# A second block's D stage ahead of the MLP, weights in ten steps, and copies moved between ScalarE and VectorE

## The chip, the cores and the metric

The kernel runs on one core of a Trainium2 chip. A core has five engines that matter here, each with its own in-order queue: TensorE (PE in the profile, its weight loads PEld), VectorE (DVE), ScalarE (ACT), GpSimd (POOL) and SyncE (SP), which only issues DMAs. The metric is the device time of one execution in microseconds; smaller is better. A time is the median of several executions.

## The reference

The input x is (8, 3072, 256) in float32. Along the sequence each of the 8 batches is filtered in the frequency domain, and the result goes through a two-layer MLP with a softplus between the layers, token by token:

```python
X = np.fft.rfft(x, axis=1)
y = np.fft.irfft(X * (filt_r + 1j * filt_i)[None], n=3072, axis=1)
h = y.reshape(8 * 3072, 256) @ w_in                      # (.., 2048)
g = np.maximum(h, 0.0) + np.log1p(np.exp(-np.abs(h)))
out = g @ w_out                                          # (.., 256)
```

The weights w_in (256 x 2048) and w_out (2048 x 256) are float64 in memory.

## The kernel before

**Arithmetic.** Every float32 operand of a matmul is split into two parts in a format that TensorE takes, a rounded high part "hi" and a rest "lo" (names ending in h and l in the profile: inh and inl, dih and dil, zh and zl, gh and gl). A product is three matmuls, hi x hi, lo x hi and hi x lo (`split_mm`, line 73). Making the parts is a copy (hi) and a subtraction (lo) on one of the elementwise engines; `hi_lo` (lines 81 to 86) is given the engine of each. The float64 weights are loaded raw and taken apart with integer and float instructions on VectorE (`weight`, lines 344 to 371: a magnitude copy on ScalarE, then five VectorE instructions, lines 356 to 368), and finished in `weight_ends` (a copy on ScalarE, line 382, and two GpSimd instructions, lines 383 and 384). There are 16 blocks of weights: 0 to 7 of w_in, 8 to 15 of w_out. `together` converts blocks in pairs, with their instructions taking turns.

**The filter** of a batch has four stages. A (12 visits): sums and differences of two halves of x, split, matmuls with the constants ca, evacuated by ScalarE into the DRAM tensor s1. B (13 visits): rows of s1 are loaded (tile bi), split, multiplied by small constants (psb in PSUM), and then by the filter on VectorE (lines 183 to 187) with a GpSimd addition (line 188). C (13 visits): split again (zh, zl), matmuls back (psc), evacuated by ScalarE (co) and written to the DRAM tensor s2. D (four visits and two y visits for each block of 512 tokens; a batch has 6 blocks): a block of s2 is loaded (tile di), split, and multiplied by constants cd with the data as the stationary operand (psd); sums and differences give y, whose parts are the tiles yT, the input of the MLP. `engines(blk)` names the engines of the splits in D: ScalarE with VectorE for batch 0's block 0, ScalarE with GpSimd for block 1, VectorE with GpSimd elsewhere.

**The MLP** works in steps: a step is one block of 512 tokens and 256 of the 2048 hidden columns; there are 8 steps to a block, 48 to a batch, 384 in all (`STEPS`). The first 16 steps take blocks 0 and 1 of batch 0 in turn, four steps each, so that the second half of the weights is needed later. `mm1` computes h (12 matmuls) into one of two PSUM buffers, and ScalarE takes it through three activations in place in the tile s (Abs, line 287; Exp, 288; Ln, 289). `soft` adds max(h, 0) on VectorE (line 296), copies to gh (line 298: on ScalarE for the 48 steps of batch 0, on VectorE later) and subtracts to gl (line 300); the five VectorE instructions of a weight conversion are laid between these three. `mm2` adds the products with w_out into the PSUM tile o, of which there is one buffer, two steps behind; after the last step of a block (and after half a block for the first two) o is evacuated into ob: one half by VectorE (line 324), the other by ScalarE (line 325), or, at the end of the first two blocks, by two VectorE additions.

**Order.** The order of every engine's instructions is written out by hand (a manual schedule). Batch 0 begins with its own A, B and C ahead of the MLP (`first_a`, `first_bc`) and D of block 0 (`first_d`). Then each step has two slots, q = 2s and 2s + 1: mm1 and the ends of a weight in the first, mm2 of step s - 2 and soft in the second; each slot then does the visits listed for it in `slots`. The D visits of a block lie in slots of the block before it; A, B and C of batch b + 1 in the steps of batch b (for batch 1 B and C come one to each free slot, later about two to three). `Run.ahead` issues loads up to 8 slots and splits up to 4 slots ahead of a visit, as far as buffers allow. `WEIGHTS` lists the weight blocks that are converted in each of the first steps; a block is loaded two steps earlier into a buffer that `TAGS` takes from the ring of another tile ("ob" by default; each has 2 buffers, "in" 3), on SP's queue, which waits where the buffer is still in use.

Of the kernel before, what the change touches and what calls it, by code (L numbers as in the profile page):

```python
# [38 lines left out]
STEPS = [(g, 4 * half + i) for half in range(2) for g in range(2) for i in range(4)]  # L39
STEPS += [(g, i) for g in range(2, NB * NBLK) for i in range(NSTEP)]  # L40

WEIGHTS = (9,), (10,), (11,), (4,), (5,), (6,), (7,), (12,), (13,), (14,), (), (15,)

TAGS = {3: "ca", 8: "ca", 5: "ca", 6: "ca", 12: "cd", 7: "in", 13: "in", 14: "in", 15: "in"}

START, END = 480, 504

# [4 lines left out]
def fft_mlp(ctx: ExitStack, tc: tile.TileContext, x, fr, fi, ca, ca0, cb, cc, cd, w_in, w_out, out):  # L52
    nc = tc.nc
# [41 lines left out]
    class Batch:  # L95
# [31 lines left out]
        def a_prep(self, i):  # L127
            self.a_sum(i)
            st = self.t.pop(("as", i))
            self.t["ap", i] = hi_lo(st, P, "in", nc.scalar if self.b == 1 else nc.vector, nc.gpsimd)  # L130

        def a_mm(self, i):
            _, cat = self.t.pop(("a", i))
# [29 lines left out]

        def b_prep(self, u):
            p = self.filled(u)
            hi_eng, lo_eng = self.engines(0)
            src = self.t["b", u][0]
            self.t["bp", u] = hi_lo(src[:p], p, "in", hi_eng, lo_eng if u < 3 or u % 2 else nc.gpsimd)

# [23 lines left out]

        def c_mm(self, u):
            if u == 0:
                self.s2 = dram.tile([2, P, N2, D], F32, tag="s2", name="s2")
            p = self.rows(u)
            zs = self.t.pop(("z", u))
            ps = ps_f.tile([P, 512], F32, tag="f", name="psc")
            if u:  # L200
                split_mm(ps, [cc_sb[:, 0, k] for k in range(2)], zs)
            else:
                for j in range(2):
                    s = slice(256 * j, 256 * j + 256)
                    split_mm(ps[:, s], [cc_sb[:, 1 - j, k] for k in range(2)], [zs[k][:, s] for k in range(2)])
            co = work.tile([P, 512], F32, tag="ao", name="co")
            nc.scalar.activation(out=co[:p], in_=ps[:p], func=AF.Copy)
            nc.scalar.dma_start(
                out=self.s2.rearrange("h m n d -> (m n) h d")[120 * u:120 * u + p],
                in_=co[:p].rearrange("p (h d) -> p h d", h=2),  # L210
            )

        def e_load(self, blk):
            cdt = work.tile([P, 2, 2, 2, P], F32R, tag="cd", name="cd")
# [3 lines left out]
        def d_load(self, i):  # L218
            blk = i // 4
            if ("e", blk) not in self.t:  # L220
                self.e_load(blk)
            dt = work.tile([P, 2, 2, D], F32, tag="di", name="di")
            for h in range(2):
                nc.sync.dma_start(out=dt[:, h], in_=self.s2[h, :, 2 * blk:2 * blk + 2, :])
            self.t["d", blk] = dt, self.t.pop(("e", blk))

        def d_prep(self, i):
            blk, j, c = i // 4, i % 2, i // 2 % 2
            if c == 0:
                dt = self.t["d", blk][0]  # L230
                self.t["dp", blk, j] = hi_lo(dt[:, :, j], P, "di", *self.engines(blk), (2, D))

        def d_mm(self, i):

# [57 lines left out]
    def soft(s, between):  # L292
        h, a = g_of.pop(s)
        hi = mlp.tile([P, 2, 512], F32R, tag="gh", name="gh")
        lo = mlp.tile([P, 2, 512], F32R, tag="gl", name="gl")
        nc.vector.scalar_tensor_tensor(out=a, in0=h, scalar=0.0, in1=a, op0=ALU.max, op1=ALU.add)  # L296
        next(between, None)
        copy(nc.scalar if s < NBLK * NSTEP else nc.vector, hi, a)
        next(between, None)
        nc.vector.tensor_sub(out=lo, in0=a, in1=hi.bitcast(F32))  # L300
        for _ in between:
            pass
        g_of[s, "g"] = hi, lo

    def mm2(s):
        g, i = STEPS[s]
        part = NSTEP // 2 if g < 2 else NSTEP
        gs = g_of.pop((s, "g"))
        if i % part == 0:
            state["o"] = ps_o.tile([P, 2, 512], F32, tag="o", name="o")  # L310
        o = state["o"]
        for h in range(2):
            for t in range(2):
                split_mm(
                    o[:, h],
                    [wo[k][:, 2 * i + t, 128 * h:128 * h + 128] for k in range(2)],
                    [gs[k][:, t] for k in range(2)],
                    i % part == 0 and t == 0,
                    i % part == part - 1 and t == 1,
                )  # L320
        if i % part == part - 1:
            if i < part or part == NSTEP:
                ob = work.tile([P, 2, 512], F32, tag="ob", name="ob")
                nc.vector.tensor_copy(out=ob[:, 0], in_=o[:, 0])
                nc.scalar.activation(out=ob[:, 1], in_=o[:, 1], func=AF.Copy)  # L325
            else:
                ob = state.pop(g)
                for h in range(2):
                    nc.vector.tensor_add(out=ob[:, h], in0=o[:, h], in1=ob[:, h])
        if i == part - 1 and i < NSTEP - 1:  # L330
            state[g] = ob
        elif i == NSTEP - 1:
            b, blk = divmod(g, NBLK)
            nc.sync.dma_start(out=out[b, blk].rearrange("h p t -> p h t"), in_=ob)
# [119 lines left out]
    NG = NB * NBLK  # L454
    LA, PA, LAG, GAP = 8, 4, 2, 4
    slots = [[] for _ in range(2 * NSTEP * NG)]
    for g in range(NG - 1):
        base = 2 * NSTEP * g
        for at, p in zip((4, 7, 8, 8, 11, 12) if g else (1, 2, 3, 4, 5, 6), d_visits(g + 1)):
            slots[base + at].append(p)  # L460
    for b in range(NB - 1):
        base = 2 * NSTEP * NBLK * b
# [58 lines left out]
    def first_bc():  # L521

        bt = batches[0]
        bt.done += "a" * N2
        for u, ft in enumerate([filter_load(u) for u in range(3)]):
            bt.b_load(u, ft)
        together((0, 1))
        weight_ends()
        bt.b_prep(0)
        for i in range(NU + 2):  # L530
            if i + 1 < NU:
                bt.b_prep(i + 1)
            if i < NU:
                bt.b_mm(i)
            if i + 3 < NU:
                bt.b_load(i + 3)
            if i == 1:
                bt.e_load(0)
                dt = work.tile([P, 2, 2, D], F32, tag="di", name="di")
                bt.t["d", 0] = dt, bt.t.pop(("e", 0))  # L540
            if i in (3, 6, 9):
                weight_load((2, 8, 3)[i // 3 - 1])
            if 0 < i <= NU:
                bt.z_mm(i - 1)
            if i >= 2:
                bt.c_mm(i - 2)
            if i in (NU - 2, NU + 1):

                r = slice(0, 100) if i < NU else slice(100, P)
                for h in range(2):  # L550
                    nc.sync.dma_start(out=dt[r, h], in_=bt.s2[h, r, :2, :])
        bt.done += "c" * NU

    def first_d():

        batches[0].d_prep(0)
        batches[0].d_prep(1)
        for _, k, i in d_visits(0):
            getattr(batches[0], f"{k}_mm")(i)
        together((8, 3))  # L560

    with tc.manual_schedule():
        nc.scalar.preload_act_table_set("natural_log_exp_and_others")
        with tc.tile_pool(name="first", bufs=1, **other) as first_pool:

            s1 = first_pool.tile([P, N2 * 512 + END], F32, name="s1f")[:, :N2 * 512]
            batches[0].s1 = s1.rearrange("p (n c) -> p n c", n=N2)
            own.update({k: first_pool.tile([P, 512, 2], U32, name=f"raw{k}") for k in (0, 1, 2)})
            with tc.tile_pool(name="start", bufs=2, **other) as start:
                first_a(batches[0].s1, start)  # L570
            first_bc()
            together((2,))
            weight_ends()
        late = ctx.enter_context(tc.tile_pool(name="late", bufs=1, **other))
        wo = late.tile([P, 32 * D + END], F32R, name="wo")[:, :32 * D].rearrange("p (k f d) -> k p f d", k=2, d=D)
        mlp = ctx.enter_context(tc.tile_pool(name="mlp", bufs=2, **other))
        run = Run(slots, 2)
        run.ahead(-4)
        for k in WEIGHTS[0] + WEIGHTS[1]:
            weight_load(k)  # L580
        first_d()
        for q in range(len(slots)):
            run.ahead(q)
            s = q // 2
            if q % 2 == 0:
                mm1(s)
                weight_ends()
            else:
                if s >= LAG:
                    mm2(s - LAG)  # L590
                soft(s, chain(*(weight(k) for k in (WEIGHTS[s] if s < len(WEIGHTS) else ()))))
                for k in WEIGHTS[s + 2] if s + 2 < len(WEIGHTS) else ():
                    weight_load(k)
            run.do(q)
        for s in range(NSTEP * NG - LAG, NSTEP * NG):
            mm2(s)
# [116 lines left out]
```

## Time and profile before

| | |
|---|---|
| time, median of 3 runs | 2539.15 us (2538.78 to 2539.96) |
| the profiled execution | 2542.45 us |
| its span | 2540.3 us |
| mean granted clock of TensorE | 0.98 |
| busy: PE, VectorE, ScalarE, GpSimd | 2447.8, 1994.2, 1556.0, 739.0 us |
| matmuls | 11232 |
| traffic with DRAM | 173.87 MB read, 72.35 MB written |

A row of the profile names the engine and the line of the kernel, the operation, the tile that it writes and those that it reads (out<-in), the shape, and the count. A line can be that of a helper: line 73 is every split matmul, lines 79 and 77 are `copy` on VectorE and ScalarE, line 85 is the subtraction of `hi_lo`. In rows in order of time the first two numbers are the start in the span and the duration in us; in brackets stands the time for which the engine was idle before, and what released it. In grouped rows the busy time and the mean of one in ns follow the bar, then the idle time ahead of them with its releasers. PE's busy time counts matmuls whose ends are modelled.

### The profile page before, as it was taken

The page shows a single profiled execution, that of the slowest core. Times are in us where ns is not written, and L with a number is a line of the kernel's source. Part 1 is how long each engine was busy: PE and PEld are TensorE (multiplying, and loading weights), DVE is VectorE, ACT ScalarE, POOL GpSimd, SP SyncE. Part 2 cuts the span into 40 slices and gives each one's busy share as a digit, 9 for nine tenths or more (in the row PEclk, how much of TensorE's full clock was granted, in tenths as well). Part 3 has the DMA queues.
Part 4 walks back from the last instruction along what each step waited for, and adds up shares of the span by engine and source line. Part 5 has one row for each costly group of instructions (what it writes and reads, how often), then busy time and mean ns, then how long its engine had stood idle before and what let it go on. Part 6 is the DMA issues. An engine that isn't in the chain of part 4 may idle for free.

```text
span 2540.3 us, 30979 instructions
## 1 busy us (share of the span) xinstructions
PE 2447.8 (96%) x11232; PEld 2029.5 (80%) x11232; DVE 1994.2 (79%) x2497; ACT 1556.0 (61%) x1810; POOL 739.0 (29%) x606
## 2 busy tenths in 40 slices
PE   5678899999999999999999999999999999999999
PEld 3467778788888888888888888888888888888887
DVE  7786775788878897789878888688887899766665
ACT  4577677666656666666666566566665666665555
POOL 4444341333214331233313333143222433111110
PEclk7789999999999999999999999999999999999999
DMA  7434433333224331343223432233422533111100
GB/s 262 125 109 148 128 99 98 117 112 109 71 75 152 114 100 52 116 137 109 81 81 117 133 87 83 90 129 101 123 64 71 172 108 92 41 42 34 42 17 17
DMA packets 144024, 251.38 MB, mean 99 GB/s; under 512 B 12736, under 2 KB 60160, under 8 KB 143872
## 3 DMA queue, kind: packets, MB, share of 16 engines
q1 hardware_dynamic: 91520, 151.36, 18.7%
q0 software_dynamic: 14112, 50.86, 6.8%
q10 hardware_dynamic: 38240, 47.20, 5.9%
q8 instruction: 88, 1.44, 0.2%
q14 instruction: 64, 0.52, 0.1%
HBM read 173.87 MB, written 72.35 MB: 97 GB/s over the span
## 4 chain that ended last, share of the span: by engine, by line
PE 86%; ACT 3%; DVE 3%; issue 1%; DMA 0%; POOL 0%; ACTq 0%; SPq 0%; DVEq 0%; POOLq 0%
PE h L73 38%; PE o L73 38%; PE psd L243 3%; PE psc L73 2%; PE psb L73 2%; PE psa L73 2%; ACT gh L77 1%; DVE s L296 1%; ACT s L288 1%; ACT s L287 1%; ACT s L289 0%; DVE gl L300 0%; ACT inh L77 0%; DVE inh L79 0%; DVE t L183 0%
## 5 line engine op out<-in xcount | busy, mean ns | idle before, releaser
L73 PE MATMUL h<-yT,wi 128*128 128x512 f32 x4608 | 1122.1, 392 | 16.4 <-ACT yT L77 8.6
L73 PEld LDWEIGHTS h<-yT,wi 128*128 128x128 f32 x4608 | 862.2, 190 | 193.4 <-ACT yT L77 9.5
L73 PE MATMUL o<-gh,wo 128*128 128x512 f32 x3072 | 951.6, 391 | 6.0 <-ACT ob L325 6.0
L287 ACT ACTIVATE s<-h 128x1024 f32<-128x1024 f32 x384 | 394.5, 1027 | 637.6 <-PE h L73 591.1
L73 PEld LDWEIGHTS o<-gh,wo 128*128 128x128 f32 x3072 | 568.6, 188 | 118.6 <-ACT ob L325 7.2
L296 DVE SCALAR_TENSOR_TENSOR s<-h,s 128x1024 f32<-128x1024 f32 x384 | 467.9, 1219 | 191.7 <-ACT s L289 190.1
L73 PE MATMUL o<-gl,wo 128*128 128x512 f32 x1536 | 598.7, 390 | 0.6 <-DVE gl L300 0.6
L300 DVE TENSOR_TENSOR gl<-s,gh 128x1024 fp32r<-128x1024 f32 x384 | 473.5, 1233 | 75.8 <-ACT gh L77 43.9
L288 ACT ACTIVATE s<-s 128x1024 f32<-128x1024 f32 x384 | 407.8, 1062 | 12.2
L289 ACT ACTIVATE s<-s 128x1024 f32<-128x1024 f32 x384 | 407.6, 1062 | 12.2
L73 PEld LDWEIGHTS o<-gl,wo 128*128 128x128 f32 x1536 | 289.0, 188 | 62.4 <-DVE gl L300 1.0
L269 POOL TENSOR_TENSOR yT<-y,yT 128x512 fp32r<-128x512 f32 x94 | 126.3, 1344 | 613.4 <-DVE yT L79 608.0
L79 DVE CAST gh<-s 128x1024 fp32r<-128x1024 f32 x336 | 276.6, 823 | 31.6 <-DVE s L296 0.9
L188 POOL TENSOR_TENSOR t<-t,t 128x512 f32<-128x512 f32 x104 | 150.6, 1448 | 408.5 <-DVE t L187 290.3
L85 POOL TENSOR_TENSOR inl<-bi,inh 128x512 fp32r<-128x512 f32 (+2 forms) x96 | 127.4, 1327 | 267.4 <-issue 100.0
L85 POOL TENSOR_TENSOR dil<-di,dih 128x512 fp32r<-128x512 f32 x94 | 123.2, 1311 | 201.9 <-DVE dih L79 139.2
L255 DVE TENSOR_TENSOR sd<-psd,ev 128x256 f32<-128x256 f32 x192 | 80.5, 420 | 120.5 <-ACT ev L254 120.5
L85 POOL TENSOR_TENSOR inl<-st,inh 128x512 fp32r<-128x512 f32 x84 | 116.3, 1384 | 165.6 <-DVE inh L79 137.7
L85 DVE TENSOR_TENSOR zl<-t,zh 128x512 fp32r<-128x512 f32 x104 | 86.8, 835 | 46.5 <-ACT zh L77 44.2
L243 PE MATMUL psd<-cd,dih 128*128 128x256 f32 x384 | 100.6, 284 | 5.9 <-ACT dih L77 5.8
L77 ACT ACTIVATE zh<-t 128x512 fp32r<-128x512 f32 x104 | 65.1, 626 | 63.5 <-POOL t L188 58.3
L243 PE MATMUL psd<-cd,dil 128*128 128x256 f32 x384 | 101.5, 286 | 0.8 <-DVE dil L85 0.8
(70 smaller groups left out, 1855.0 us busy)
## 6 DMA issues: line engine op xcount, KB each, us to landing
ft<-in_fr SPq DMA_DIRECT2D x104, 256.0 KB
x<-in_x SPq DMA_DIRECT2D x48, 512.0 KB
ca<-in_ca POOLq DMA_DIRECT2D x48, 512.0 KB, 4.8
cd<-in_cd POOLq DMA_DIRECT2D x48, 512.0 KB, 4.0
out<-ob SPq DMA_DIRECT2D x48, 512.0 KB
di<-s SPq DMA_DIRECT2D x94, 256.0 KB
s<-co ACTq DMA_DIRECT2D x96, 240.0 KB
s<-ao ACTq DMA_DIRECT2D x84, 256.0 KB
```

The costliest lines, as they stand in the source:

```text
L73: nc.tensor.matmul(out=ps, lhsT=lhs[a], rhs=rhs[b], start=first and k == 0, stop=last and k == 2)
L77: nc.scalar.activation(out=out, in_=in_, func=AF.Copy)
L79: eng.tensor_copy(out=out, in_=in_)
L85: lo_eng.tensor_sub(out=lo[:p], in0=src, in1=hi[:p].bitcast(F32))
L188: nc.gpsimd.tensor_add(out=t1, in0=t1, in1=t2)
L243: nc.tensor.matmul(out=ps[:, h].rearrange("p k n -> p (k n)"), lhsT=ds[k][:, h, 128 * c:128 * c + 128], rhs=cdt[:, h, j].rearrange("p k n ...
L269: lo_eng.tensor_sub(out=lo[:, c], in0=y, in1=hi[:, c].bitcast(F32))
L287: nc.scalar.activation(out=a, in_=h, func=AF.Abs)
L288: nc.scalar.activation(out=a, in_=a, func=AF.Exp, scale=-1.0)
L289: nc.scalar.activation(out=a, in_=a, func=AF.Ln, bias=1.0)
L296: nc.vector.scalar_tensor_tensor(out=a, in0=h, scalar=0.0, in1=a, op0=ALU.max, op1=ALU.add)
L300: nc.vector.tensor_sub(out=lo, in0=a, in1=hi.bitcast(F32))
```

## The change

The first D stage takes two blocks instead of one, both ahead of the MLP; the D visits of block 1 leave the slots 1 to 6. Weight 3 is converted as a pair with weight 2 ahead of D (before, weight 2 alone), and weights 8 and 9 as a pair behind D (before, 8 and 3). The weights left, 10, 11, 4 to 7 and 12 to 15, are converted one in each of steps 0 to 9 (before, 9 to 15 and 4 to 7 over steps 0 to 11, step 10 having none). Weight 11 takes a buffer of the "in" ring. The loads of block 1's di and cd and of weights 9, 10 and 11 are issued at the end of `first_bc`. The gh copy is on ScalarE for steps 0 to 15 only. A's hi copy of batch 1 goes from ScalarE to VectorE, and B's hi copy of batch 1 from VectorE to ScalarE. Both halves of o are evacuated by ScalarE for batch 0's blocks where they are copied. In s2 the two halves h of a row now lie together, so that C writes 2 KB rows and a block's di is one DMA instead of two.

```diff
-WEIGHTS = (9,), (10,), (11,), (4,), (5,), (6,), (7,), (12,), (13,), (14,), (), (15,)
-
-TAGS = {3: "ca", 8: "ca", 5: "ca", 6: "ca", 12: "cd", 7: "in", 13: "in", 14: "in", 15: "in"}
+WEIGHTS = (10,), (11,), (4,), (5,), (6,), (7,), (12,), (13,), (14,), (15,)
+
+TAGS = {3: "ca", 8: "ca", 5: "ca", 6: "ca", 12: "cd", 11: "in", 7: "in", 13: "in", 14: "in", 15: "in"}
...
-            self.t["ap", i] = hi_lo(st, P, "in", nc.scalar if self.b == 1 else nc.vector, nc.gpsimd)
+            self.t["ap", i] = hi_lo(st, P, "in", nc.vector, nc.gpsimd)
...
-            hi_eng, lo_eng = self.engines(0)
+            hi_eng, lo_eng = nc.scalar if self.b == 1 else self.engines(0)[0], self.engines(0)[1]
...
-                self.s2 = dram.tile([2, P, N2, D], F32, tag="s2", name="s2")
+                self.s2 = dram.tile([P, N2, 2, D], F32, tag="s2", name="s2")
...
-            nc.scalar.dma_start(
-                out=self.s2.rearrange("h m n d -> (m n) h d")[120 * u:120 * u + p],
-                in_=co[:p].rearrange("p (h d) -> p h d", h=2),
-            )
+            nc.scalar.dma_start(out=self.s2.rearrange("m n h d -> (m n) (h d)")[120 * u:120 * u + p], in_=co[:p])
...
-            for h in range(2):
-                nc.sync.dma_start(out=dt[:, h], in_=self.s2[h, :, 2 * blk:2 * blk + 2, :])
+            nc.sync.dma_start(out=dt, in_=self.s2[:, 2 * blk:2 * blk + 2])
...
-                self.t["dp", blk, j] = hi_lo(dt[:, :, j], P, "di", *self.engines(blk), (2, D))
+                self.t["dp", blk, j] = hi_lo(dt[:, j], P, "di", *self.engines(blk), (2, D))
...
-        copy(nc.scalar if s < NBLK * NSTEP else nc.vector, hi, a)
+        copy(nc.scalar if s < 2 * NSTEP else nc.vector, hi, a)
...
-                nc.vector.tensor_copy(out=ob[:, 0], in_=o[:, 0])
+                copy(nc.scalar if g < NBLK else nc.vector, ob[:, 0], o[:, 0])
...
-    for g in range(NG - 1):
+    for g in range(1, NG - 1):
         base = 2 * NSTEP * g
-        for at, p in zip((4, 7, 8, 8, 11, 12) if g else (1, 2, 3, 4, 5, 6), d_visits(g + 1)):
+        for at, p in zip((4, 7, 8, 8, 11, 12), d_visits(g + 1)):
...
-                for h in range(2):
-                    nc.sync.dma_start(out=dt[r, h], in_=bt.s2[h, r, :2, :])
+                nc.sync.dma_start(out=dt[r], in_=bt.s2[r, :2])
         bt.done += "c" * NU
+        bt.d_load(4)
+        for k in (9, *WEIGHTS[0], *WEIGHTS[1]):
+            weight_load(k)

     def first_d():

-        batches[0].d_prep(0)
-        batches[0].d_prep(1)
-        for _, k, i in d_visits(0):
-            getattr(batches[0], f"{k}_mm")(i)
-        together((8, 3))
+        for g in range(2):
+            batches[0].d_prep(4 * g)
+            batches[0].d_prep(4 * g + 1)
+            for _, k, i in d_visits(g):
+                getattr(batches[0], f"{k}_mm")(i)
+        together((8, 9))
...
-            together((2,))
+            together((2, 3))
             weight_ends()
...
+        first_d()
         run = Run(slots, 2)
-        run.ahead(-4)
-        for k in WEIGHTS[0] + WEIGHTS[1]:
-            weight_load(k)
-        first_d()
```

## The prediction

> **What bounds the kernel now.** I read the page first: its line of PE's granted clock falls below 9 only in the first two of 40 slices. Then I cut the span at the first ScalarE activation (line 287, one per MLP step; below, "Abs(s)" is that of step s) of steps 0, 10, 16, 50, 96 and 144, and asked for each engine's busy time between these points (the columns: stretch, length, then PE, weight loads, VectorE, ScalarE, GpSimd, each with its count, the granted clock, DMA share, GB/s), and for line 287 alone, whose counts are the numbers of steps.
>
> ```profile
> PEclk7789999999999999999999999999999999999999
> ```
> ```profile
> 0.00:104.90 104.90, 60.20 (x186) 40.22 (x187) 79.65 (x110) 45.54 (x70) 44.14 (x40) 0.69 0.71 229
> 104.90:182.00 77.10, 57.73 (x240) 45.82 (x239) 68.22 (x84) 56.65 (x69) 36.52 (x30) 0.89 0.24 83
> 182.00:231.30 49.30, 43.84 (x203) 35.48 (x202) 33.15 (x44) 35.10 (x46) 19.11 (x18) 0.96 0.51 160
> 231.30:473.40 242.10, 224.78 (x1008) 183.78 (x1008) 162.61 (x204) 165.39 (x194) 77.65 (x61) 0.97 0.33 104
> 473.40:760.50 287.10, 287.10 (x1339) 240.18 (x1339) 234.96 (x296) 174.82 (x202) 84.50 (x69) 1.00 0.33 101
> 760.50:1060.40 299.90, 299.90 (x1405) 251.29 (x1405) 247.80 (x311) 183.36 (x212) 90.70 (x74) 1.00 0.33 102
> ```
> ```profile
> 104.90:182.00 77.10, 10.15 (x10) 0.89 0.24 83
> 182.00:231.30 49.30, 6.06 (x6) 0.96 0.51 160
> 231.30:473.40 242.10, 34.55 (x34) 0.97 0.33 104
> ```
>
> From 473 us on PE is never idle and its clock is 1.00: a whole batch of 48 steps takes 299.9 us, 6.25 us a step, and nothing in this change takes work from PE. So only what lies before 473 us can move. There the steps take 7.7, 8.2 and 7.1 us. PE is idle for 19.4, 5.5 and 17.3 us of the three stages, and loses (1 - clock) of each besides: 8.5, 2.0 and 7.3 us. At full clock PE's own work in them is 49, 42 and 217.5 us. What ended most of PE's idle time in the first two of these stages (us in total, times, longest):
>
> ```profile
> PE h L73 <- ACT yT L77: 6.5, 1, 6.5
> PE o L73 <- ACT ob L325: 5.0, 2, 4.8
> PE h L73 <- DVE s L296: 3.8, 2, 2.3
> PE h L73 <- POOL wi L384: 3.7, 1, 3.7
> ```
>
> The largest is the second block's yT, which the D visits in slots 1 to 6 bring late; then the release of o by the evacuation; then the release of h by VectorE's sum, and a weight block converted just in time.
>
> **The front, up to Abs(0): + 7.5 us.** D's own pace comes from block 0:
>
> ```profile
> 88.52 0.69 DVE L360 SCALAR_TENSOR_TENSOR raw<-raw,p 128x512 uint32<-128x512 uint32 x1 [2.36 <-ACT m L355]
> 90.43 0.69 DVE L368 SCALAR_TENSOR_TENSOR raw<-raw,p 128x512 f32<-128x512 uint32 x1
> 91.90 1.15 ACT L77 ACTIVATE dih<-di 128x512 fp32r<-128x512 f32 x2 [1.26 <-DMA di<-s]
> 92.56 1.98 DVE L85 TENSOR_TENSOR dil<-di,dih 128x512 fp32r<-128x512 f32 x2 [1.44 <-ACT dih L77]
> 97.56 0.27 PE L243 MATMUL psd<-cd,dil 128*128 128x256 f32 x1
> 98.24 1.23 PE L73 MATMUL h<-yT,wi 128*128 128x512 f32 x3 [0.40 <-ACT yT L77]
> 100.41 0.63 ACT L77 ACTIVATE yT<-y 128x512 fp32r<-128x512 f32 x1 [1.67 <-DVE y L263]
> 101.68 0.76 DVE L356 TENSOR_SCALAR p<-raw 128x512 uint32<-128x512 uint32 x2
> 102.78 3.10 POOL L85 TENSOR_TENSOR dil<-di,dih 128x512 fp32r<-128x512 f32 x2 [8.89 <-ACT dih L77]
> 104.94 1.03 ACT L287 ACTIVATE s<-h 128x1024 f32<-128x1024 f32 x1 [1.73 <-PE h L73]
> 107.63 1.28 DVE L368 SCALAR_TENSOR_TENSOR raw<-raw,p 128x512 f32<-128x512 uint32 x2
> 108.83 1.21 DVE L296 SCALAR_TENSOR_TENSOR s<-h,s 128x1024 f32<-128x1024 f32 x1
> 144.77 2.88 PE L73 MATMUL h<-yT,wi 128*128 128x512 f32 x12
> ```
>
> Weights 2 and 3 are now converted as a pair ahead of block 0's D. VectorE ended weight 2 alone at 90.43 + 0.69 = 91.12, having waited for ScalarE's magnitude copy until 88.52, which hides the first of weight 3's five instructions. The other four add two of 0.69 and the halves of 0.76 and 1.28: 2.4 us, so dil starts at 93.5 instead of 92.56: + 0.9. Block 1's dih copies reuse block 0's two buffers and stand behind its last yT copy on ScalarE, so they start at 100.41 + 0.63 + 0.9 = 101.9. From the first dih to the last D matmul block 0 needed 97.83 - 91.90 = 5.9 us; block 1's dil runs on GpSimd, 3.10 for two instead of 1.98, of which I take 0.5 as lasting. PE is free for mm1(0) at 108.3. It has been half idle, so it starts at half clock, as its 3 matmuls at 98.24 did (1.23, so 4.9 for twelve against 2.88 at full clock); I take 4.1 us, warm again on the way. Abs(0) follows at 112.4 instead of 104.94: + 7.5. Bounds: + 5 (PE warm, VectorE not late) and + 11 (Abs(0) behind the two magnitude copies of weights 8 and 9, GpSimd slow). VectorE starts the pair (8, 9) only when block 1's y is done, at about 110.3, and ends it at 117.5, by the 7.2 us that (8, 3) took from 101.68 to 108.91. So the first softplus sum moves from 108.83 to 117.5, and Abs(1), behind gh(0) on ScalarE, stands 7.4 us behind Abs(0).
>
> The queues that things are moved past:
>
> ```profile
> 90.31 0.84 SPq L224 DMA_DIRECT2D di<-s  x2
> 91.20 28.15 SPq L341 DMA_DIRECT2D raw<-in_w_out  x3
> ```
>
> SP's third weight load (weight 11) stood some 28 us behind the buffer of weight 9. Now 11 has a buffer of another ring, so 9, 10 and 11 go out at once at about 91, behind block 1's di load; what hides their traffic from it is the 10 us until its dih. Weight 4 waits on SP for weight 9's buffer instead, until GpSimd's add, about 121; it is converted two steps later, and nothing urgent stands behind it. On GpSimd's queue block 1's cd load is issued ahead of the subtractions of weights 2 and 3 instead of behind weight 2's, when that engine has nothing to do. If di or cd came late, block 1's D would, and mm1(0) with it. At nothing.
>
> **Steps 0 to 9: 77.1 becomes 62.8 us.**
>
> ```profile
> 142.20 1.03 ACT L287 ACTIVATE s<-h 128x1024 f32<-128x1024 f32 x1 [3.18 <-PE h L73]
> 147.72 1.01 ACT L287 ACTIVATE s<-h 128x1024 f32<-128x1024 f32 x1
> 172.97 1.01 ACT L287 ACTIVATE s<-h 128x1024 f32<-128x1024 f32 x1
> ```
>
> Each of the ten steps holds one conversion. Steps 4 to 8 of the old kernel are of this kind with no D visit: (172.97 - 142.20)/5 = 6.15 us, one evacuation included; the shortest took 5.5, where ScalarE's chain of three activations, VectorE's sum and the gh copy is the bound. 7.4 + 9 x 6.15 = 62.8; bounds 57 and 69.5 (nine of 5.5 or of 6.9). The evacuation's first half goes to ScalarE, behind the same matmul; ScalarE stops waiting for VectorE's queue there, the longest wait being the 4.8 us above, which the 6.15 leaves out. Nothing more for it.
>
> **Steps 10 to 15: 49.3 becomes 42 us.** No conversion is left here, and batch 1's A visits begin. PE needs 42 by the row above; ScalarE loses the inh copies and its waits for them, so I take PE's bound, 7.0 a step; 40 (the row's edges cut matmuls of both neighbours) to 46.
>
> **Steps 16 to 49: 242.1 becomes 228 us.**
>
> ```profile
> L300 DVE TENSOR_TENSOR gl<-s,gh 128x1024 fp32r<-128x1024 f32 x34 | 42.1, 1240 | 37.9 <-ACT gh L77 37.8
> L79 DVE CAST inh<-bi 128x512 fp32r<-128x512 f32 (+1 forms) x13 | 9.9, 764 | 0.1
> ```
> ```profile
> L77 ACT ACTIVATE gh<-s 128x1024 fp32r<-128x1024 f32 x32 | 33.9, 1059 | 49.7 <-DVE s L296 41.9 <-PE o L73 4.1 <-PE psc L73 2.8
> ```
> ```profile
> L79 DVE CAST gh<-s 128x1024 fp32r<-128x1024 f32 x309 | 257.4, 833 | 29.1 <-DVE s L296 0.9
> ```
> ```profile
> PE psb L73 <- DVE t L187: 3.8, 3, 2.0
> PE psc L73 <- DVE t L187: 3.3, 2, 1.7
> ```
>
> ScalarE gives up 33.9 us of gh copies and the 49.7 us it waited ahead of them; VectorE takes 32 x 0.83 = 26.7 us (the mean over 309 steady steps), but no longer waits 37.8 us for gh, and it hands 9.9 us of inh casts to ScalarE. So VectorE's queue gets shorter by some 20 us. PE's 217.5 us are the floor; 24.6 us of loss stand above it. The B and C visits come one to every free slot here, and PE's waits for VectorE in them (7.1 us in the two rows) shrink with that queue but needn't vanish. I leave 10 of the 24.6: 228. Bounds 221 and 240.
>
> One rule speaks against this. The Trainium skill, "SBUF — State Buffer", section "Who interferes with whom", says that a VectorE copy or cast from SBUF to SBUF can take the port pair that it shares with GpSimd for the whole instruction, and that whichever comes second is blocked. The trace doesn't contradict it, since its casts vary, but in batches whose PE never stops their mean is 0.83 us. By that mean the sum stands; by the rule at its worst the first rival below would come, whose price is from rows.
>
> **s2's layout.** C writes rows of twice the length, and D loads a block by one DMA instead of two: one SP issue of 0.42 us fewer a block, in a queue that loads steps ahead. That lookahead hides it either way. At nothing.
>
> **Sum.** Against the profiled execution's 2542.45 (span 2540.3): + 7.5 - 14.3 - 7.3 - 14.1 = - 28.2, so 2514.2; it stood 3.3 above the median of 2539.15, so the forecast is **2511 us**. All low bounds together give 2495 (- 5 + 20 + 9 + 21 = 45 us less), all high ones 2537.
>
> **Rivals.** *VectorE becomes the bound in steps 16 to 49 (slower).* For: one zl took 2.38 us while GpSimd worked, and stretches of that stage keep it busy for 87%:
>
> ```profile
> 78.01 2.38 DVE L85 TENSOR_TENSOR zl<-t,zh 128x512 fp32r<-128x512 f32 x1
> 345.00:365.00 20.00, 17.85 (x77) 14.12 (x77) 17.40 (x22) 13.84 (x17) 9.18 (x7) 1.00 0.36 110
> ```
>
> At 2.4 us for each of 32 casts VectorE would hold 162.6 + 77 - 10 + 42 (its other idle time, 242.1 - 162.6 - 37.8) = 271 us, 29 more than the stage has. The rest wins 14, so this decides from casts of 1.95 us on; at 2.4 the time is 2539 - 14 + 29 = 2554. Against: the mean of 0.83. 5%. *The B and C chain binds, not gh:* PE's waits there are for VectorE's t and the preparation with two buffers, and keep their length; the stage stays at 242: 2525. 13%. *The conversions bind steps 0 to 9:* each step as long as now (7.7), the stalls only renamed: + 7.5 - 7.3 - 14.1, so 2525. For: VectorE is busy for 68 of 77 us there; against: steps 4 to 8. 11%. *The edit does not do what it says:* the late yT is late through its conversions, which only move, gh had slack, and all comes out as before, 2539. 3%.
>
> **Chances and range.** The forecast has 68%, with 2498 to 2518 for its own. With most of the two cases at 2525 the range is 2497 to 2526. About 0.2% (5 us) can be told from no change: faster 0.92, within it 0.03, slower 0.05.
>
> **What would show it.** Right: Abs(0) at 110 to 116; no wait of h for yT in steps 0 to 9, and these in about 63 us; Abs(10) near 175; no gl waiting for ScalarE's gh from step 16 on, and 34 steps from there in 221 to 240 us; from step 50 to the end the same time as before within 1 us. Wrong: PE waits for VectorE's t above 15 us in that stage, a gh cast above 1.2 us on average there, or Abs(10) after 182.

## The result and the profile after

The changed kernel takes 2520.74 us (median of 4 runs, 2519.59 to 2521.07) against 2539.56 us before (2538.78 to 2541.01): a ratio of 0.9924, 95% interval 0.9907 to 0.9942. That is faster by 18.8 us, two thirds of the 28 us that were forecast: within the stated range of 2497 to 2526, but 2.7 us above the 2498 to 2518 that the forecast gave for its own case. The profiled execution took 2520.59 us, with a span of 2518.7. Every time here and below is the median of the fast executions of a kernel; two far longer ones, 4968.68 us of "evacuation back" and 9459.98 us of "the same, gh for 10 steps", are left out.

The span after, cut at the first activations of the same steps (0, 10, 16, 50, 96, 144; columns as in the prediction):

```profile
0.00:112.90 112.90, 64.68 (x204) 45.20 (x205) 83.87 (x121) 49.03 (x78) 51.56 (x44) 0.70 0.68 218
112.90:178.40 65.50, 56.87 (x231) 44.55 (x230) 63.90 (x75) 54.99 (x66) 33.19 (x27) 0.95 0.27 97
178.40:222.50 44.10, 38.49 (x183) 31.85 (x182) 34.41 (x44) 29.52 (x36) 18.09 (x17) 0.96 0.51 163
222.50:451.70 229.20, 221.34 (x1020) 182.88 (x1019) 187.16 (x224) 143.01 (x174) 80.58 (x61) 0.99 0.34 106
451.70:738.50 286.80, 286.80 (x1339) 240.21 (x1339) 237.24 (x300) 174.84 (x202) 84.45 (x69) 1.00 0.34 104
738.50:1038.40 299.90, 299.90 (x1406) 251.42 (x1405) 248.08 (x312) 183.32 (x212) 90.59 (x74) 1.00 0.34 102
```

| stretch | before | forecast | after |
|---|---|---|---|
| up to Abs(0) | 104.9 | 112.4 | 112.9 |
| steps 0 to 9 | 77.1 | 62.8 | 65.5 |
| steps 10 to 15 | 49.3 | 42 | 44.1 |
| steps 16 to 49 | 242.1 | 228 | 229.2 |
| steps 50 to 95 | 287.1 | the same | 286.8 |

From step 50 on nothing has moved: a batch is 299.9 us as before. All of the change lies ahead of it, and every stretch went the way it was forecast, each falling a little short.

The front, in order of time (ScalarE, GpSimd, VectorE, PE):

```profile
92.94 1.15 ACT L77 ACTIVATE dih<-di 128x512 fp32r<-128x512 f32 x2 [0.26 <-DMA di<-s]
102.06 0.63 ACT L77 ACTIVATE yT<-y 128x512 fp32r<-128x512 f32 x1 [1.73 <-DVE y L259]
102.60 1.13 ACT L77 ACTIVATE dih<-di 128x512 fp32r<-128x512 f32 x2
...
111.81 1.21 ACT L351 ACTIVATE m<-raw 128x512 f32<-128x512 f32 x2
112.92 1.03 ACT L283 ACTIVATE s<-h 128x1024 f32<-128x1024 f32 x1
...
119.66 1.01 ACT L283 ACTIVATE s<-h 128x1024 f32<-128x1024 f32 x1
```
```profile
117.44 1.22 DVE L292 SCALAR_TENSOR_TENSOR s<-h,s 128x1024 f32<-128x1024 f32 x1
```
```profile
108.87 6.12 PE L73 MATMUL h<-yT,wi 128*128 128x512 f32 x24
```

Block 1's dih copies start behind block 0's last yT copy at 102.6, PE is free for the MLP at 108.87, Abs(0) comes at 112.92, the first softplus sum at 117.44 and Abs(1) 6.7 us behind Abs(0). The forecast had 101.9, 108.3, 112.4, 117.5 and 7.4.

What ended PE's waits in steps 0 to 9:

```profile
PE h L73 <- DVE s L292: 4.5, 3, 3.7
PE o L73 <- ACT ob L321: 3.9, 2, 2.8
```

The waits for yT (6.5 us) and for a weight block (3.7 us) are gone. VectorE is now busy for 63.9 of the 65.5 us of these steps (the second row of the first view), where it was busy for 68.2 of 77.1. VectorE's waits in steps 16 to 49:

```profile
DVE s L292 <- ACT s L285: 14.2, 9, 2.7
DVE sd L251 <- ACT ev L250: 9.5, 6, 2.4
DVE zl L85 <- ACT zh L77: 6.5, 5, 2.8
```

Of the 37.8 us that gl waited for ScalarE's gh one wait of 1.2 is left, that of step 15's gl. VectorE is busy for 187 of 229 us there, where it was busy for 163 of 242.

### The profile page after: what moved, and what is told of

Read it like the earlier page. It is cut to its first block, busy times and chain, and to the rows that moved or that the text cites. A ratio compares the mean times of both kernels' runs of the same rounds, so it can differ in the third digit from the quotient of the medians.

```text
span 2518.7 us, 30955 instructions
## 1 busy us (share of the span) xinstructions
PE 2442.4 (97%) x11232; PEld 2029.2 (81%) x11232; DVE 2022.0 (80%) x2522; ACT 1529.8 (61%) x1785; POOL 744.9 (30%) x606
## 4 chain that ended last, share of the span: by engine, by line
PE 86%; DVE 5%; ACT 1%; issue 1%; POOL 0%; DVEq 0%; ACTq 0%; POOLq 0%
PE h L73 39%; PE o L73 38%; PE psd L239 3%; PE psc L73 2%; PE psb L73 2%; PE psa L73 2%; DVE s L292 1%; DVE gl L296 1%; DVE gh L79 1%; DVE inh L79 0%; ACT s L283 0%; ACT s L284 0%; DVE st L125 0%; ACT gh L77 0%; DVE dih L79 0%
## 5 line engine op out<-in xcount | busy, mean ns | idle before, releaser
L296 DVE TENSOR_TENSOR gl<-s,gh 128x1024 fp32r<-128x1024 f32 x384 | 474.3, 1235 | 42.5 <-ACT gh L77 7.1
L79 DVE CAST gh<-s 128x1024 fp32r<-128x1024 f32 x368 | 304.9, 829 | 35.1 <-DVE s L292 1.4
L188 POOL TENSOR_TENSOR t<-t,t 128x512 f32<-128x512 f32 x104 | 149.9, 1441 | 409.0 <-DVE t L187 285.5
L239 PE MATMUL psd<-cd,dih 128*128 128x256 f32 x384 | 102.3, 288 | 10.8 <-ACT dih L77 10.7
```

Of the source, the lines that this page charges most:

```text
L79: eng.tensor_copy(out=out, in_=in_)
L188: nc.gpsimd.tensor_add(out=t1, in0=t1, in1=t2)
L239: nc.tensor.matmul(out=ps[:, h].rearrange("p k n -> p (k n)"), lhsT=ds[k][:, h, 128 * c:128 * c + 128], rhs=cdt[:, h, j].rearrange("p k n ...
```

## The experiments

Each kernel was timed against the kernel before on the same chip; "gain" is the difference of the two medians, and the ratio is taken over their runs. Beside the last eight kernels the kernel before took 2.1 to 2.3 us more than beside the change, which was not timed again there, so a difference of that size between rows shows nothing. Stages are compared by their lengths in the profiles, because Abs(0) itself varies from profile to profile: from 112.9 to 115.1 us, 114.2 on average, among the nine kernels whose instructions up to there are the same. The change's own profile is the earliest of the nine.

| kernel | time (us) | before beside it | gain | ratio, 95% interval |
|---|---|---|---|---|
| the change | 2520.74 | 2539.56 | 18.8 | 0.9924 (0.9907 to 0.9942) |
| gh on ScalarE for 48 steps | 2528.70 | 2539.90 | 11.2 | 0.9954 (0.9940 to 0.9969) |
| one D block ahead | 2524.67 | 2539.90 | 15.2 | 0.9941 (0.9925 to 0.9958) |
| hi copies back | 2529.12 | 2539.90 | 10.8 | 0.9959 (0.9944 to 0.9974) |
| evacuation back | 2523.10 | 2539.90 | 16.8 | 0.9929 (0.9913 to 0.9946) |
| s2 layout back | 2520.51 | 2541.67 | 21.2 | 0.9919 (0.9904 to 0.9934) |
| weights' order back | 2520.23 | 2541.88 | 21.7 | 0.9916 (0.9901 to 0.9931) |
| gh on ScalarE for 10 steps | 2517.69 | 2541.67 | 24.0 | 0.9907 (0.9891 to 0.9924) |
| weight ends behind mm2 | 2520.29 | 2541.67 | 21.4 | 0.9919 (0.9904 to 0.9934) |
| A four slots earlier | 2513.59 | 2541.67 | 28.1 | 0.9892 (0.9877 to 0.9907) |
| the same, gh for 10 steps | 2512.49 | 2541.88 | 29.4 | 0.9883 (0.9866 to 0.9899) |
| A two slots earlier, gh for 10 | 2513.60 | 2541.88 | 28.3 | 0.9890 (0.9875 to 0.9905) |
| four edits together | 2516.19 | 2541.88 | 25.7 | 0.9897 (0.9880 to 0.9913) |

Stage lengths in the profiles (us), the first activation of one step to that of another, by the exact starts (so that a last digit can differ from the rows above). Steps 22 to 39 took 130.7 us or 129.1 in kernels that are the same there, so 1.6 us of a difference in them can be chance.

| kernel | Abs(0) | 0 to 10 | 10 to 16 | 16 to 22 | 22 to 40 | 40 to 50 |
|---|---|---|---|---|---|---|
| before | 104.9 | 77.1 | 49.3 | 43.0 | 135.1 | 63.9 |
| the change | 112.9 | 65.5 | 44.0 | 39.9 | 130.7 | 58.6 |
| gh on ScalarE for 48 steps | 113.7 | 65.6 | 44.0 | 41.6 | 130.4 | 62.8 |
| one D block ahead | 106.6 | 76.1 | 43.9 | 39.9 | 130.7 | 58.6 |
| hi copies back | 113.4 | 64.9 | 47.6 | 42.7 | 133.5 | 58.6 |
| evacuation back | 114.6 | 66.5 | 43.9 | 39.9 | 130.6 | 58.6 |
| s2 layout back | 112.4 | 65.5 | 44.3 | 39.9 | 130.7 | 58.6 |
| weights' order back | 110.2 | 65.6 | 46.8 | 39.9 | 129.1 | 58.6 |
| gh on ScalarE for 10 steps | 114.5 | 65.5 | 40.3 | 40.5 | 130.7 | 58.6 |
| weight ends behind mm2 | 115.1 | 65.6 | 43.6 | 39.9 | 129.1 | 58.6 |
| A four slots earlier | 114.8 | 71.9 | 43.5 | 38.2 | 118.9 | 58.6 |
| the same, gh for 10 steps | 114.5 | 72.0 | 41.7 | 38.5 | 119.1 | 58.6 |
| A two slots earlier, gh for 10 | 114.3 | 66.8 | 42.5 | 39.5 | 125.1 | 58.6 |
| four edits together | 115.4 | 70.7 | 43.9 | 38.3 | 119.1 | 58.6 |

**Undoing one part: gh.**

```diff
-        copy(nc.scalar if s < 2 * NSTEP else nc.vector, hi, a)
+        copy(nc.scalar if s < NBLK * NSTEP else nc.vector, hi, a)
```

> The changed kernel with one edit undone: the gh copy stays on ScalarE for all 48 steps of batch 0. Theory (the gh copy on ScalarE holds both queues in steps 16 to 49): these 34 steps go from 229 back to about 240 us, VectorE waits for gh some 35 us there again, time about 2531. Rival (gh had slack, and the shorter queue came from the inh copies and the evacuation): the 34 steps stay within 231 us and the time within 2519 to 2523.

Measured: 2528.70 us, 7.6 us of the gain gone. Steps 16 to 49 take 234.8 us instead of 229.2, half of what the theory asked; VectorE's wait for gh is back in full:

```profile
DVE gl L296 <- ACT gh L77: 39.1, 33, 1.5
```

The 5.6 us lie in steps 16 to 21 (1.7) and 40 to 49 (4.2). In steps 22 to 39, with the B and C visits, there are none (130.4 against 130.7): there the wait is only swapped for the cast. So the copy had no slack, but its price was paid in other steps than expected.

**One D block.**

```diff
-        for g in range(2):
+        for g in range(1):
             batches[0].d_prep(4 * g)
...
-    for g in range(1, NG - 1):
+    for g in range(NG - 1):
```

(with the old slots 1 to 6, and block 1's loads where they were, ahead of D)

> The changed kernel with one edit undone: only block 0's D ahead of the MLP, block 1's D visits back in slots 1 to 6; the order of the weights stays new. Theory (block 1's late yT costs more than its D ahead): the first step's activation comes back from 113 to about 107, a wait of h for yT of several us is back in steps 0 to 9, and the time is 2524 to 2528. Rival (the D ahead costs at the front what it saves, and the weights do the rest): 2517 to 2521.

Measured: 2524.67 us, 3.6 us of the gain gone. Abs(0) is at 106.6, and steps 0 to 9 take 76.1 us again. PE's waits there:

```profile
PE h L73 <- ACT yT L77: 6.5, 1, 6.5
PE psd L239 <- DVE sd L251: 4.4, 1, 4.4
PE o L73 <- ACT ob L321: 2.3, 1, 2.3
```

The theory holds: the block costs 6.3 us at the front (112.9 - 106.6; 7.6 by the average of the nine fronts) and brings 10.6 in steps 0 to 9. By time alone the two kernels can't be told apart, as their intervals overlap; the stages and the wait decide. With the new order of the weights and without D ahead, yT is exactly as late as before.

**The hi copies of batch 1.**

```diff
-            self.t["ap", i] = hi_lo(st, P, "in", nc.vector, nc.gpsimd)
+            self.t["ap", i] = hi_lo(st, P, "in", nc.scalar if self.b == 1 else nc.vector, nc.gpsimd)
...
-            hi_eng, lo_eng = nc.scalar if self.b == 1 else self.engines(0)[0], self.engines(0)[1]
+            hi_eng, lo_eng = self.engines(0)
```

> The changed kernel with one edit undone: in batch 1 A's hi copy on ScalarE and B's on VectorE as before. Theory (both copies stand on the longer queue of their stage): steps 10 to 15 take 2 us more, steps 16 to 49 3 us more, time about 2525. Rival (these copies have slack): 2520 to 2522, the stages unchanged within 1 us.

Measured: 2529.12 us, 8.0 us of the gain gone, about twice what was expected, and as much as for gh within the noise. Steps 10 to 15 take 3.6 us more, 16 to 21 and 22 to 39 2.8 more each. In steps 10 to 21 the 12 copies of A on ScalarE, and on VectorE in the changed kernel:

```profile
L77 ACT ACTIVATE inh<-st 128x512 fp32r<-128x512 f32 x12 | 7.6, 633 | 17.2 <-DVE st L123 12.0 <-DVE st L125 3.2 <-ACT ao L141 2.0
```
```profile
L79 DVE CAST inh<-st 128x512 fp32r<-128x512 f32 x12 | 10.3, 861 | 1.1
```

The copy itself is longer on VectorE (861 ns against 633). What it saves is ScalarE's idle time before it: 17.2 us, of which ScalarE waited 15.2 for the sum that VectorE makes just ahead, with the next step's activations behind it. The copies of A and B were only undone together. The 6.4 us of steps 10 to 21 lie where A's run; the 2.8 of steps 22 to 39, where B's run, are little more than chance can bring there.

**The evacuation.**

```diff
-                copy(nc.scalar if g < NBLK else nc.vector, ob[:, 0], o[:, 0])
+                nc.vector.tensor_copy(out=ob[:, 0], in_=o[:, 0])
```

> The changed kernel with one edit undone: the first half of o is evacuated by VectorE again in batch 0. Theory (the release of o waits for VectorE's queue, then stalls PE): PE's waits of o for ob rise from 3.9 to 6 to 9 us, time 2523 to 2526. Rival (ScalarE's queue is as late, because the end of a weight conversion ahead of it waits for VectorE too): the waits stay at about 4 us, time 2520 to 2522.

Measured: 2523.10 us, and steps 0 to 9 take 1.0 us more. PE's wait there:

```profile
PE o L73 <- ACT ob L321: 6.4, 2, 3.3
```

The wait rises from 3.9 to 6.4 us as the theory has it, but the steps lose only 1 us: about as much as VectorE's busy time rises (63.9 to 64.8 us). The 2.0 us of gain that are gone are within the two intervals.

**The layout of s2, and the order of the weights.** The first puts the two DMAs a block back. The second:

```diff
-WEIGHTS = (10,), (11,), (4,), (5,), (6,), (7,), (12,), (13,), (14,), (15,)
+WEIGHTS = (9,), (10,), (11,), (4,), (5,), (6,), (7,), (12,), (13,), (14,), (), (15,)
...
-        together((8, 9))
+        together((8, 3))
...
-            together((2, 3))
+            together((2,))
```

> The changed kernel with s2 in its old layout (two DMAs for each block's di, C writing pieces of half the length). Theory (the lookahead hides it): 2519.5 to 2522.5, every stage within 1 us. Rival (shorter writes and reads bring the first D forward): the first step's activation 1 us later and 2522 to 2524.

> The changed kernel with the old order of the weights: 2 alone ahead of D, 8 and 3 as a pair behind it, 9 to 15 and 4 to 7 over steps 0 to 11, weight 11 in its old ring; both D blocks stay ahead of the MLP. The other single edits, undone one by one, already add up to the whole gain (5.6 + 8.6 + 0.8 + 0.2 us from the first step to step 50, and 3.9 us of time for D). Theory (the order of the weights is worth nothing by itself): 2519 to 2523. Rival (conversions that end at step 9 and not at 11 shorten steps 10 to 15): these steps 3 us longer, time 2524 to 2527.

Measured: 2520.51 and 2520.23 us; neither can be told from the change. The layout moves no stage by more than 0.5 us. The old order of the weights costs 2.8 us in steps 10 to 15, which the rival had, but the time that the rival put on it did not come: its Abs(0) is the earliest of those with both D blocks ahead (110.2, with one conversion fewer before D, 2.7 us below the change's, of which the front's spread may be a part), and steps 22 to 39 are 1.6 shorter, which is within chance.

**gh for ten steps.** `s < 10` in the place of `s < 2 * NSTEP`.

> The changed kernel with the gh copy on ScalarE for steps 0 to 9 only, as long as weights are converted, instead of 0 to 15. Theory (the gh copy on ScalarE makes VectorE wait wherever no conversion loads VectorE): steps 10 to 15 go from 44.0 to 41 us, time about 2518. Rival (A's copies bind these steps and VectorE is as long): 44 us or more, 2520 to 2523.

Measured: 2517.69 us; steps 10 to 15 take 40.3 us instead of 44.0, steps 16 to 21 0.6 more: 3.2 us from step 0 to step 50. The theory holds. PE's waits for psa there, behind sd in VectorE's queue, shrink from 2.0 to 0.5 us and those behind inl from 1.3 to 0.7.

**The end of a conversion behind mm2.**

```diff
             if q % 2 == 0:
                 mm1(s)
-                weight_ends()
             else:
                 if s >= LAG:
                     mm2(s - LAG)
+                weight_ends()
```

> The changed kernel with the end of a weight conversion (the copy on ScalarE and the two GpSimd instructions) issued behind mm2 and its evacuation instead of behind mm1. Theory (the excess of steps 0 to 9 over the forecast is the evacuation standing behind that copy, which waits for VectorE): PE's waits of o for ob fall from 3.9 to below 1.5 us, these steps take 62 to 63.5 us instead of 65.5, time 2517 to 2519. Rival (the next step is paced by VectorE's queue anyway): waits of o gone but the steps still 65 us, 2520 to 2522.

Measured: 2520.29 us, steps 0 to 9 at 65.6 us. Both sides were wrong about the wait, which stayed at 3.9 us. ScalarE around the first evacuation:

```profile
147.51 1.01 ACT L283 ACTIVATE s<-h 128x1024 f32<-128x1024 f32 x1
148.55 1.06 ACT L284 ACTIVATE s<-s 128x1024 f32<-128x1024 f32 x1
149.64 1.06 ACT L285 ACTIVATE s<-s 128x1024 f32<-128x1024 f32 x1
150.61 0.58 ACT L77 ACTIVATE ob<-o 128x512 f32<-128x512 f32 x1
151.08 0.59 ACT L321 ACTIVATE ob<-o 128x512 f32<-128x512 f32 x1
151.56 0.67 ACT L378 ACTIVATE wi<-raw 128x512 fp32r<-128x512 f32 x1
152.12 0.67 ACT L351 ACTIVATE m<-raw 128x512 f32<-128x512 f32 x1
152.68 1.06 ACT L77 ACTIVATE gh<-s 128x1024 fp32r<-128x1024 f32 x1
```

ScalarE has no gap here: the copy of the weight's end now stands behind the evacuation, and Abs of the next step comes as late as before. Its own work for this step, both halves of the evacuation included, fills the time, and over the ten steps VectorE is busy for 63.9 of 65.6 us. So PE's wait for o is a symptom: these steps are not paced by that copy's place.

**A four free slots earlier.** `(14, 3, 59)` in the place of `(18, 3, 59)`: B and C have 30 free slots for their 26 visits.

> The changed kernel with batch 1's A visits starting four free slots earlier, so that its B and C visits have 30 slots for 26 instead of 26. Theory (PE's waits in steps 22 to 39 come from B and C following each other in every slot, with two buffers for the parts): steps 22 to 39 go from 130.7 to 126 us, time about 2516 if steps 10 to 15 take no more. Rival (VectorE's load binds them, whatever the spacing): steps 22 to 39 change by less than 1.5 us, 2519 to 2523.

Measured: 2513.59 us, a gain of 28.1 us where the change has 18.8; the two intervals only touch. Steps 22 to 39 take 118.9 us instead of 130.7, where 126 had been expected. PE's waits there, in the changed kernel and in this one:

```profile
PE psc L73 <- DVE t L187: 4.0, 2, 2.4
PE psb L73 <- DVE t L187: 1.3, 2, 1.1
PE psb L73 <- POOL inl L85: 1.3, 1, 1.3
PE psb L73 <- ACT co L207: 0.8, 2, 0.4
```
```profile
PE psb L73 <- ACT co L207: 0.4, 1, 0.4
```

And the engines' busy time in that stretch, again first the changed kernel, then this one (columns as above):

```profile
262.40:393.10 130.70, 123.38 (x549) 100.47 (x548) 114.17 (x135) 82.20 (x103) 49.27 (x35) 0.99 0.31 93
```
```profile
268.50:387.40 118.90, 118.44 (x538) 97.65 (x536) 103.52 (x125) 78.56 (x99) 41.53 (x32) 1.00 0.34 104
```

PE's idle time falls from 7.3 to 0.5 us and its clock is full again. The rival, that VectorE's load binds whatever the spacing, is refuted: over steps 0 to 49 VectorE's work is nearly the same (285.5 us before the edit, 281.7 after), and its share of this stretch is 87% in both. What the edit changed is how the work is spread. It gives B and C more room and takes 10.7 us of VectorE's work out of the stretch, and these two were not separated. Part of the 11.8 us is paid in steps 0 to 9, which take 71.9 us instead of 65.5, with VectorE busy for 70.0 of them instead of 63.9:

```profile
114.80:186.70 71.90, 62.25 (x247) 48.53 (x246) 70.02 (x83) 56.42 (x67) 38.93 (x31) 0.91 0.34 113
```

From step 0 to step 50 the kernel wins 7.6 us.

**Edits together.** A four slots earlier with gh for ten steps; the same with A two slots earlier; and the first of these with the late ends of the conversions and this front:

```diff
         for g in range(2):
             batches[0].d_prep(4 * g)
             batches[0].d_prep(4 * g + 1)
+            if g:
+                together((8,))
             for _, k, i in d_visits(g):
                 getattr(batches[0], f"{k}_mm")(i)
-        together((8, 9))
+        together((9,))
```

> The changed kernel with both: A visits four free slots earlier, and gh on ScalarE for steps 0 to 9 only. Theory (separate causes: the spacing of B and C, and ScalarE's queue in steps 10 to 15): the two gains add, 7.1 + 3.0 us, time 2510 to 2512. Rival (A's earlier visits already use what gh leaves in steps 10 to 15): 2513 to 2515.

> As the kernel before it, but A only two free slots earlier, so that its loads don't wait for buffers of the weights in steps 7 to 10 (where four slots cost 6 us). Theory (spacing against buffers): steps 0 to 9 back to 65.5 us, steps 22 to 39 half way (125 us), time 2510 to 2514. Rival (the spacing alone decides): half the gain of four slots, 2514 to 2516.

> A four free slots earlier, gh on ScalarE for steps 0 to 9 only, the ends of the conversions behind mm2, and weight 8 converted between block 1's split and its D visits, with weight 9 alone behind them. Theory (VectorE sits idle for 2.7 us ahead of block 1's D): the second step's activation 1 to 2 us nearer to the first, time 2508 to 2511. Rival (block 1's D then waits for VectorE and mm1(0) comes later by as much): within 1.5 us of the run without the last two edits.

Measured: 2512.49, 2513.60 and 2516.19 us. The first is the fastest by its median, 29.4 us before the old one, a ratio of 0.9883 whose interval (0.9866 to 0.9899) lies wholly below that of the change, but overlaps that of A's shift alone. Its time lies between theory and rival; the stages decide. From step 0 to step 50 it is only 1.4 us shorter than with A's shift alone (329.8 against 331.2), where gh alone had brought 3.2: the rival's side, as steps 10 to 15 show (41.7 against 40.3). With two slots the stages come as the theory had them (66.8 and 125.1), and the sum is no better. In the last kernel both sides missed: it is 3.7 us slower than the first, where the theory had it faster and the rival within 1.5 us; the intervals overlap. Abs(1) stands at 121.2, where the first has 120.9, so filling VectorE's idle time ahead of block 1's D brought nothing. PE in its front:

```profile
108.96 0.58 PE L239 MATMUL psd<-cd,dih 128*128 128x256 f32 x1 [1.79 <-DVE sd L251]
...
110.84 7.32 PE L73 MATMUL h<-yT,wi 128*128 128x512 f32 x24
```

Block 1's D waits for VectorE, which converts weight 8 in that time, and mm1(0) begins 8.1 us behind the start of block 1's dih copies (102.73), where the first kernel needs 6.3 (103.90 to 110.17): the rival's mechanism. Of the 3.2 us between the two spans, 0.9 lie ahead of Abs(0), 0.9 in steps 0 to 49 and 1.4 behind them; where these 1.4 come from stays open.

## Why the prediction was right, and where it fell short

**The range.** The measured time lies outside what the forecast gave for its own case. It lies in the stated range because that was widened for two rivals at 2525, so that the number falls inside is in part luck. What was right is the way, and the stages in which the time was won.

**The front** was right to 0.5 us, and that is in part luck too. D's own pace from block 0, the place of the dih copies behind the last yT, and the pair (8, 9) as what holds the first softplus sum are as forecast. But mm1(0) took 3.4 us and not 4.1: nearer to the 2.88 of twelve matmuls at full clock than to the 4.9 at half clock. Abs(0) then stood 0.6 us behind it, directly behind ScalarE's two magnitude copies of weights 8 and 9 (the row at 111.81), which the prediction had only in its upper bound. VectorE began that pair at 111.2 and not 110.3, and took 6.4 us for it and not 7.2. The two errors cancel in each case. And this profile is the earliest of nine fronts: their average, 114.2, is 1.8 us above the forecast.

**Steps 0 to 9** were forecast at 62.8 us and took 65.5. The causes were right: the waits for yT and for the weight block are gone, and the run with one D block brings yT's 6.5 us back. The term that was too small is the nine steps at 6.15. Seven of them are as forecast, 42.5 us from Abs(2) to Abs(9), 6.07 each:

```profile
127.46 1.00 ACT L283 ACTIVATE s<-h 128x1024 f32<-128x1024 f32 x1
...
169.93 1.01 ACT L283 ACTIVATE s<-h 128x1024 f32<-128x1024 f32 x1
178.47 1.01 ACT L283 ACTIVATE s<-h 128x1024 f32<-128x1024 f32 x1
```

The first of them (Abs(1) to Abs(2)) took 7.8, and the last, with the second evacuation and a split of block 2 in VectorE's queue, 8.5. The row that the 6.15 came from had one evacuation and left the other out; two steps of ten with work of their own make 4.0 us, of which the other eight give 1.3 back. In the first of the two VectorE ran without a gap, and its gl took 2.32 us (1.28 on average in steps 16 to 49) while GpSimd finished weight 9:

```profile
120.36 2.32 DVE L296 TENSOR_TENSOR gl<-s,gh 128x1024 fp32r<-128x1024 f32 x1
```
```profile
119.85 1.75 POOL L379 TENSOR_TENSOR raw<-raw,wo 128x512 f32<-128x512 f32 x1
121.68 1.90 POOL L380 TENSOR_TENSOR wo<-raw 128x512 fp32r<-128x512 f32 x1
```

Beneath this lies VectorE's load. It is busy for 63.9 us in these steps, more than the 62.8 forecast for the whole stage: the prediction priced a step by the spacing of old steps and set no term for VectorE's work. In the runs with both D blocks ahead these steps are 1.6 to 1.9 us longer than that work, whether it is 63.3 us (hi copies back), 63.9 (the change), 64.8 (evacuation back), 65.0 (A two slots earlier) or 70.0 (A four slots earlier); only the four edits together leave more, 67.3 of 70.7 us. So the rival that the conversions bind these steps, which pointed at VectorE, had the mechanism, and its price, steps as long as before, was wrong.

**Steps 10 to 15** were put at PE's bound of 42 us and took 44.1. The step that failed is that PE would bind them: gh is still on ScalarE there, PE waited 5.6 us (2.3 of it for the softplus sum), and in the run with gh for ten steps they took 40.3, 3.7 us less, of which 0.6 came back in the next six. That run also shows that 42 was no bound: PE's work between these two points is 183 matmuls, where the old row had 203. The copy could have left ScalarE six steps sooner.

**Steps 16 to 49** were forecast at 228 and took 229.2, but half for another reason than the one given. The prediction let VectorE's shorter queue carry the gain, most of it through gh, and left the B and C steps a part of their waits. The runs: gh 5.6 us, none of it in steps 22 to 39; the hi copies 5.6, of which the prediction had counted only VectorE's share. So the rival that the B and C chain binds, not gh, was right for 18 of the 34 steps, where undoing gh changed nothing that can be seen and the earlier A won 11.8 us, and wrong for the rest. The rival of a VectorE that becomes the bound did not come: the casts took 881 ns on average there, dearer than the 833 of the steady steps but far from 1.95 us:

```profile
L79 DVE CAST gh<-s 128x1024 fp32r<-128x1024 f32 x34 | 29.9, 881 | 3.3
```

**At nothing** stood the layout of s2, and nothing can be seen of it. The moves in the queues of SP and GpSimd, also at nothing, were not undone by themselves. The evacuation, also at nothing, is worth 1 us in the steps.

**The sum.** Of the 9.7 us between forecast and median, the stages make 6.3 (28.2 against the 21.9 by which the profiled executions differ, 2542.45 and 2520.59). The rest is the base: the profiled execution of before stood 3.3 us above its median, and I carried its savings over whole, while that of after stands 0.15 below its own. A part of what I saw as waste in the old profile may have been that one execution's own. Two small slips change nothing: the row of the granted clock is below 9 in three slices and not two, and the low bounds add up to 2494 and not 2495.

Undone one by one, the parts are worth, from step 0 to step 50: D ahead 10.4 us, the hi copies 8.6, gh 5.6, the order of the weights 1.3, the evacuation 0.8, the layout 0.2. They add up to 26.9 of the 29.7 by which these steps got shorter, so the parts interact little. Against that stands the front, 8.0 us longer: by the profiles D's block costs 6.3 there and the order of the weights 2.7, each uncertain by the fronts' spread of 2.2. Less what it costs at the front, D brings 4.1 us, and the largest net shares are the copies that changed engines: the two hi copies and gh.

## What to carry to other kernels

Where two engines hand a tile to and fro in in-order queues, count what a copy makes its engine wait for, with all that stands behind it, before its own length: two copies that swapped engines won 8.6 us from step 0 to step 50, 6.4 of them in the twelve steps of the one that is 230 ns longer in its new place, where ScalarE no longer stopped for VectorE's sum. Work that a late result depends on may be moved ahead of a loop even if it delays the loop's start, if what it costs there (6 to 8 us here) can be read from a neighbour of its kind and what it saves (10 us) is a stall with a name. And when a stage's waits all point to one busy engine, try the spacing of the visits before the engine's load: with VectorE's work in the fifty steps nearly the same, starting four slots earlier took PE's idle time in 18 of them from 7.3 to 0.5 us. The room has a price elsewhere: where VectorE was already busy for 63.9 of 65.5 us, the visits moved there cost 6.4 us of the 11.8 that they won.

## What the runs showed of the hardware

The first GpSimd subtraction of the weights ahead of D took 3.76 us, where it took 1.55 at that place before. VectorE ran four instructions with two inputs in SBUF back to back beside the first 2.6 us of it (GpSimd, then VectorE):

```profile
92.45 3.76 POOL L379 TENSOR_TENSOR raw<-raw,wi 128x512 f32<-128x512 f32 x1 [6.64 <-ACT wi L378]
```
```profile
92.55 1.29 DVE L364 SCALAR_TENSOR_TENSOR raw<-raw,p 128x512 f32<-128x512 uint32 x2
93.75 1.29 DVE L85 TENSOR_TENSOR dil<-di,dih 128x512 fp32r<-128x512 f32 x2
```

Before, VectorE was idle for most of that subtraction. Its two dil (at 92.56, shown in the prediction) began behind the start of GpSimd's next instruction, an addition, and it was they that were long, 1.98 us:

```profile
90.72 1.55 POOL L383 TENSOR_TENSOR raw<-raw,wi 128x512 f32<-128x512 f32 x1 [6.29 <-ACT wi L382]
92.35 1.04 POOL L384 TENSOR_TENSOR wi<-raw 128x512 fp32r<-128x512 f32 x1
```

The Trainium skill, "SBUF — State Buffer", section "Who interferes with whom", says that a VectorE instruction with two inputs in SBUF contends with a GpSimd instruction that reads SBUF, and that issue order decides who blocks. The trace agrees that they contend: GpSimd's subtraction went from 1.55 us almost alone to 3.76 beside VectorE, and VectorE's pair from 1.98 beside GpSimd's addition to 1.29. On the order it agrees in the old kernel, where GpSimd began 0.21 us ahead; in the new one the two starts lie 0.10 us apart, too near to tell.
